# Splitting the value weights among the q products, ones by ScalarE, a padded tile of maxima and a new order at the stage borders of a transformer block

## The chip, the cores and the metric

The kernel runs on one core of a Trainium2 chip. The core has five engines that each work through a queue of their own, in order: TensorE (PE, matrix products; its loads of the stationary operand are listed as PEld), VectorE (DVE), ScalarE (ACT), GpSimd (POOL), and SyncE (SP), which here only issues DMA transfers. ACT issues a few transfers too. Engines wait for each other by semaphores. The metric is the device time of one execution in microseconds; lower is better.

## What is computed

The block is a transformer block on x of 2048 rows by 512 columns, with a condition vector c that modulates both halves. The attention has 32 heads of 16, works in 4 segments of 512 rows, and each segment also reads a memory that the earlier segments wrote.

```python
mod = (_silu(c) @ w_mod).reshape(c.shape[0], 6, 1, -1)
sa, ca, ga, sb, cb, gb = ...
h = _layernorm(x) * (1 + ca) + sa
x = x + ga * _A_ref(h, A_wq, A_wk, A_wv, A_wo, A_beta)
h = _layernorm(x) * (1 + cb) + sb
x = x + gb * _B_ref(h, B_w1, B_b1, B_w2, B_b2)

# _A_ref, for each segment s, with phi(t) = t + 1 where t > 0, else exp(t)
logits = einsum("bhqd,bhkd->bhqk", qs, ks) * scale + mask
a_dot = einsum("bhqk,bhkd->bhqd", softmax(logits), vs)
num = einsum("bhld,bhde->bhle", phi(qs), M)
den = einsum("bhld,bhd->bhl", phi(qs), z)[..., None] + 1e-6
outs.append(g * num / den + (1.0 - g) * a_dot)
M = M + einsum("bhld,bhle->bhde", phi(ks), vs)
z = z + einsum("bhld->bhd", phi(ks))
# then o @ wo

# _B_ref, with 1792 hidden columns
gelu(x @ w1 + b1) @ w2 + b2
```

The mask here is the reference's own: a key after the query gets -1e9.

## The kernel before

The whole order of the work is written out by hand (the scheduler is told to keep program order), so each engine's queue is the program's order.

**Projections, segment by segment.** `PRM["A"]` holds one string of tokens for each of the four segments, and the loop in `block_kernel` that reads it turns each token into steps. `Q0`–`Q3` and `K0`–`K3` are the q and k products of 128 columns each (48 matmuls of 512 columns in three precision terms per four products); `N0`–`N3` are segment 0's q, whose matmuls already ran, so that only their evictions are left. `V0`–`V3` are the value products. `proj` evicts a product: ACT copies it to bf16 (`parts[0]`), DVE subtracts (`r1`), ACT copies the rest (`parts[1]`), POOL makes the third part; where phi is wanted, ACT takes the exponential, POOL (DVE for the fourth k) takes a minimum, and a last DVE step, put off into `late_v`, completes it. The stores of the parts to the DRAM buffers QD and KD are put off into `late_sp` and go out on SP with the next product. `gk`/`gv` copy the high half of a weight block on ACT, `lk`/`lv` subtract the low half on DVE. `s0`–`s3`, `r`, `p0`–`p3` are the LayerNorm of the next segment's x (statistics and normalisation on DVE, the inverse root on POOL). `X` loads x, `W` loads eight blocks of w_mod on SP, `D` is one of the eight steps that multiply and add them (two on ACT, six on DVE). `Tk` transposes phi(k) on PE, `Tc` copies it on ACT, `At` transposes the normalised x, `Ah` scales it on ACT, `H` splits it on DVE, `U` updates the memory. `R` reads the memory (products dn and nu on PE, three DVE steps on dn, four ACT copies), `Rs` stores the reciprocal, `Rm` multiplies on POOL, `Ro` and `Rz` store to AMD on SP. `b` prepares the gates, with 32 small POOL memsets. `B`, in segment 3, allocates the first two stacks (`new_stack`, which writes ones into the last 32 rows of `kst`) and loads them (`load_stacks`). Products share eight PSUM banks in rotation.

**Attention.** The 32 heads of the 4 segments make 64 steps P of two heads; two steps make a group Q of four heads. For each P, PE forms the logits with the query on the partitions (line L607 and, for the small blocks, L640, L641 and the mask product L650), DVE takes their masked maxima (L610, L614) four steps ahead, `m_rows` (L666) splits a group's maxima into three bf16 terms on DVE, `m_put` turns them with one product (L671), ACT copies the result (`ms`) and sends it by DMA into three rows of `qst`, so that the second logit product (L692, keys on the partitions) comes out with the maximum subtracted. ACT takes exponentials (L707, L718), POOL masks the diagonal blocks (L695), and PE multiplies with V (`pv`, L732). Inside a step the order comes from `PRM["order"]`; positions such as `mrows`, `mput`, `mix` are offsets in tenths of a step P from the start of the group (of U, two groups, for `mix`, `olo`, `ohi`). For each U the output goes to DRAM and back (TD, dn, opk), the denominators go through RD and return spread as rbB, `mix` combines them (POOL up to U=13, DVE for 14 and 15), `o_hi` (ACT) and `o_lo` split the result, and `wo_part` multiplies with wo (L809) into the bank `mm`. `wo_out` adds x and stores rows to X2D.

**Feed-forward.** `ffn1(n)` forms one column block of 128 (L982) and applies gelu on ACT (L985); `ffn2(m)` runs four blocks behind (`AHEAD` = 4) and adds into four banks `acc` (L1068). w1 and w2 are loaded and split pair by pair: `stage_w1`, `split_w1`, `stage_w2`, `scale_w2` (w2 times the gate, DVE, L1003), `split_w2` (ACT high half L136, DVE low half L139). The first blocks and the last of the attention are interleaved by hand, with `rest(U, ...)` taking steps that are left over.

Of the kernel before, what the change touches and what calls it, by code (L numbers as in the profile page):

```python
# [8 lines left out]
F32 = mybir.dt.float32  # L9
# [3 lines left out]
ALU = mybir.AluOpType  # L13
# [28 lines left out]
 'mput': [-9, -14, -14, -14],  # L42
# [10 lines left out]
 'mixu': 14,  # L53
 'olou': 14,
# [50 lines left out]
def block_kernel(ctx: ExitStack, tc: tile.TileContext, x, wq, wk, wv, wo, betaq, betam,  # L105
# [57 lines left out]
    def transposed(pl, hp, bank, xh, s, ci, tag, bufs, hbufs=2, ds=range(KB), pss=None, lo=None):  # L163
        hs, ls = [], []
        for d in ds:
            ps = pss[d] if pss else turned(bank(), xh, d)
            h = pl.tile([128, 512], F32, tag=f"{tag}h", bufs=hbufs, name=f"{tag}h{s}_{d}")
            act.activation(h, ps, AF.Identity, bias=cols[:, ci, d:d + 1], scale=cols[:, ci + 1, d:d + 1])
            hh = hp.tile([128, 512], F32R, tag=f"{tag}hh", bufs=bufs, name=f"{tag}hh{s}_{d}")
            if tag == "C0" and s == 0 and d == 0:  # L170
                hp.tile([128, 8], F32, name="cpad1")
            hl = hp.tile([128, 512], F32R, tag=f"{tag}hl", bufs=bufs, name=f"{tag}hl{s}_{d}")
            split(hh, hl, h, lo or v)
            hs.append(hh)
            ls.append(hl)
        return hs, ls
# [7 lines left out]
    def new_stack(i, pl=None):  # L184
        for n, d in (("qst", qst), ("kst", kst)):
            a = {"name": f"{n}{i}"} if pl else {"name": f"{n}{i}", "tag": "wm", "bufs": 4}
            d[i] = (pl or wmp).tile([128, 4, 512], BF16, **a)
        (v if i < 2 else pool).memset(kst[i][96:], 1.0)
# [30 lines left out]
    with ExitStack() as pa:  # L219
# [47 lines left out]
        load_mod((0, 1), (act, sp))  # L267
        wqs = load_w(wp, wq, "wq", "phq")
# [232 lines left out]
        def proj(s, nm, g):  # L501
# [8 lines left out]
            r1 = sa.tile([128, 512], F32, tag="qkr", bufs=2, name=f"{nm}r{s}_{g}")  # L510
            act.activation(parts[0], ps, AF.Copy)
            v.tensor_tensor(out=r1, in0=ps, in1=parts[0], op=ALU.subtract)
            flush(late_v)
            if phi:
                ph = sat(f"ph{nm}", f"{nm}p{s}_{g}")
                act.activation(ph, ps, AF.Exp)
                (v if nm == "k" and g == 3 else pool).tensor_scalar(ph, ph, 1.0, None, op0=ALU.min)
                kw = {}
                if nm == "k":
                    if s not in zss:  # L520
                        zss[s] = sa.tile([128, 4], F32, tag="z", name=f"z{s}")
                    kw["accum_out"] = zss[s][:, g:g + 1]
                late_v.append(lambda: v.scalar_tensor_tensor(ph, ps, 1.0, ph, op0=ALU.add, op1=ALU.max, **kw))
                (phq if nm == "q" else phk)[s, g] = ph
# [38 lines left out]
    ce.tile([128, 16], F32, name="cpad0")  # L563
# [23 lines left out]
    with ExitStack() as pb:  # L587
# [4 lines left out]
        so.tile([128, 8], F32, name="spad")  # L592
# [3 lines left out]
        nms, nss = {}, {}  # L596

# [18 lines left out]
        def s_part(P, part):  # L616
            Q, p = P // 2, P % 2
            if p == 0 and part == 0:
                nms[Q] = sb.tile([128, 3, 16], F32, tag="nm", bufs=4, name=f"nm{Q}")
# [43 lines left out]
        def m_rows(Q):  # L663
            n = nms.pop(Q)
            for c in range(2):
                v.tensor_tensor(out=n[:, c + 1], in0=n[:, c], in1=top(n[:, c]), op=ALU.subtract)  # L666
            nss[Q] = n

        def m_put(Q):
            ns = nss.pop(Q)  # L670
            pe.matmul(mm[:48, :128], top(ns.rearrange("q c n -> q (c n)")), identb, start=True, stop=True)  # L671
            ms = sb.tile([48, 128], BF16, tag="ms", bufs=2, name=f"ms{Q}")
            copy(PRM["mse"], ms, mm[:48, :128])
            act.dma_start(qst[Q % NK][96:99], ms)
# [139 lines left out]
        def wo_x(s, b):  # L814
            xbs[s, b] = so.tile([128, D], F32, tag="xb", bufs=3, name=f"xb{s}_{b}")
            r0 = 512 * s + 128 * b
            sp.dma_start(xbs[s, b], x[r0:r0 + 128, :])
# [138 lines left out]
    with ExitStack() as pc:  # L956
# [65 lines left out]
        for b in range(3):  # L1022
            wo_x(3, b)
# [6 lines left out]
        ffn1(3)  # L1030
# [5 lines left out]
        rest(15, "mem_mix", "mix", "o_hi", "o_lo")  # L1036
        assert not [x for x in left if x[0] != "wo_x"], left
        for b in range(4):
            if b == 3:
                wo_x(3, 3)  # L1040
            wo_part(3, b, 3)
            wo_out(3, b)
        scale_w2(0)
        sostack.close()
        c2 = pc.enter_context(tc.tile_pool(name="c2", bufs=1, reuse_waits="tile"))
        w2t = {f: [c2.tile([128, D], F32R, name=f"w2{i}{f}") for i in "hl"] for f in range(FB - 1, 2, -1)}
# [34 lines left out]
        b2r = []  # L1081
        ln2_load(1)
        for n in range(AHEAD, NSEG * FB + AHEAD):
            s, f = divmod(n, FB)
            m = n - AHEAD
            if m < FB:
                split_w2(m)
# [32 lines left out]
            if n < NSEG * FB:  # L1120
                ffn1(n)
# [59 lines left out]
```

## Time and profile before

| what | us |
|---|---|
| runs before: median of 3 | 851.94 |
| runs before: lowest, highest | 850.7, 856.96 |
| profiled execution, device time | 853.31 |
| profiled execution, span from first to last instruction | 851.6 |
| ACT busy in the span | 360.4 |
| DVE busy in the span | 533.5 |
| mean granted TensorE clock | 0.986 |

The times fall into four stretches that can be told apart in the profile: projections to about 194 us, attention to about 513, the border to the feed-forward to about 555, and the feed-forward to the end. A row of the wait view names the engine that waited, its line, what it waited for, then total us, times and the longest. A timeline row gives start, duration, engine, line, operation, output and inputs, the count of merged instructions, and in brackets the idle time before it and what ended it.

### The profile page before, as it was taken

What the parts mean: (1) busy time and instruction counts of PE and PEld (TensorE: products, weight loads), DVE (VectorE), ACT (ScalarE), POOL (GpSimd) and SP (SyncE); (2) the same over time, 40 slices, a digit from 0 to 9 for tenths busy, and PEclk for the clock granted to TensorE, in tenths of its full rate; (3) what the DMA queues carried; (4) which work ended last, traced back from release to release, by engine and by line L of the source; (5) the groups of instructions that cost most, each with busy time, mean ns of one, the idle gap of its engine ahead of it and who ended that gap; (6) DMA issues with size and microseconds to landing.
All of it is one profiled execution on the core that took longest, in us unless ns stands there. A gap on an engine that the chain in (4) does not pass through costs nothing.

```text
span 851.6 us, 13418 instructions
## 1 busy us (share of the span) xinstructions
PE 818.6 (96%) x4669; PEld 552.9 (65%) x4669; DVE 533.5 (63%) x1432; ACT 360.4 (42%) x730; POOL 281.5 (33%) x449
## 2 busy tenths in 40 slices
PE   8979999988999999999999989799999999999998
PEld 4767786855443445445544547588888888888887
DVE  6586775557899987898788725677543334334213
ACT  4454545432678775676687662113211211111110
POOL 1435448145358544557858571000000000000000
PEclk9999999999799999999999999999999999999999
DMA  9854946486365576656556563733020103002001
GB/s 338 293 164 149 308 154 199 153 274 222 101 179 170 161 217 188 210 177 203 178 170 184 183 191 119 233 118 117 26 99 1 50 0 99 1 0 75 26 1 49
DMA packets 83564, 123.01 MB, mean 144 GB/s; under 512 B 14116, under 2 KB 46244, under 8 KB 82984
## 3 DMA queue, kind: packets, MB, share of 16 engines
q1 hardware_dynamic: 81000, 120.19, 44.4%
q10 hardware_dynamic: 2496, 1.97, 0.7%
q8 instruction: 36, 0.59, 0.3%
q14 instruction: 32, 0.26, 0.1%
HBM read 75.60 MB, written 46.15 MB: 143 GB/s over the span
## 4 chain that ended last, share of the span: by engine, by line
PE 72%; DVE 9%; DMA 6%; issue 5%; POOL 3%; ACT 3%; SPq 1%; ACTq 0%; POOLq 0%; DVEq 0%
PE f1b L982 17%; PE acc L1068 17%; PE pv L732 6%; PE att L692 6%; PE att L607 5%; PE mm L809 4%; DVE att L610 4%; PE q L329 3%; PE k L329 2%; PE v L482 2%; PE nu L452 1%; DMA QD<-q 1%; DMA qst<-ms 1%; PE att L650 1%; PE mp L429 1%
## 5 line engine op out<-in xcount | busy, mean ns | idle before, releaser
L610 DVE CUSTOM_DVE_ANT_0 att<-att,maskb 128x512 f32<-128x512 f32 (+2 forms) x384 | 206.7, 580 | 19.9 <-PE att L607 17.3
L707 ACT ACTIVATE pt<-att 128x512 f32<-128x512 f32 (+1 forms) x256 | 125.9, 554 | 54.9 <-PE att L692 54.3
L985 ACT ACTIVATE gt<-f1b,b1t 128x512 f32<-128x512 f32 x56 | 38.4, 688 | 249.0 <-PE f1b L982 205.5
L695 POOL TENSOR_SCALAR_AFFINE_SELECT pt<-pt 128x256 f32<-128x256 f32 x256 | 100.9, 411 | 100.1 <-ACT pt L707 71.1
L138 DVE CAST gh<-gt 128x512 fp32r<-128x512 f32 x56 | 23.8, 425 | 173.2 <-ACT gt L985 173.2
L692 PE MATMUL att<-qst,kst 99*128 99x512 bf16 (+3 forms) x512 | 108.7, 306 | 5.2 <-ACT pt L718 1.8
L607 PE MATMUL att<-kst,qst 96*128 96x512 bf16 (+2 forms) x384 | 96.8, 334 | 3.3 <-DMA qst<-QD 3.1
L1068 PE MATMUL acc<-w2h,gh 128*128 128x512 f32 (+1 forms) x224 | 87.9, 393 | 3.1 <-ACT w2h L136 3.1
L1068 PE MATMUL acc<-w2l,gh 128*128 128x512 f32 (+1 forms) x224 | 87.4, 390 | 1.0 <-DVE w2l L139 1.0
L732 PE MATMUL pv<-pt,V 128*32 128x512 f32 (+2 forms) x992 | 88.2, 442 | 0.0
L1068 PE MATMUL acc<-w2h,gl 128*128 128x512 f32 (+1 forms) x224 | 86.7, 387 | 0.0
L692 PEld LDWEIGHTS <-kst 99*128 99x128 bf16 x512 | 44.9, 99 | 58.3 <-issue 42.5
L982 PE MATMUL f1b<-hodd,w1h 128*128 128x512 f32 x224 | 74.3, 393 | 0.0
L718 ACT ACTIVATE pt<-att 128x512 f32<-128x512 f32 (+1 forms) x128 | 57.1, 509 | 23.3 <-PE att L607 19.6
L607 PEld LDWEIGHTS <-qst 96*128 96x128 bf16 x384 | 33.7, 99 | 42.9 <-issue 24.4
L151 POOL TENSOR_SCALAR crs<-cmv 128x4 f32<-128x4 f32 x4 | 1.0, 246 | 177.8 <-DVE cmv L148 177.7
L610 DVE DVE_READ_ACCUMULATOR2_ANT nm<- 128x1 f32 x384 | 54.2, 141 | 0.0
L1068 PEld LDWEIGHTS acc<-w2h,gh 128*128 128x128 f32 x224 | 42.5, 190 | 12.0 <-ACT w2h L136 3.5
L1068 PEld LDWEIGHTS acc<-w2l,gh 128*128 128x128 f32 x224 | 42.4, 189 | 10.7 <-DVE w2l L139 1.8
L1068 PEld LDWEIGHTS acc<-w2h,gl 128*128 128x128 f32 x224 | 42.4, 189 | 9.0
L982 PEld LDWEIGHTS f1b<-hodd,w1h 128*128 128x128 f32 x224 | 42.1, 188 | 9.1
L732 PEld LDWEIGHTS pv<-pt,V 128*32 128x32 f32 x992 | 22.2, 108 | 36.7 <-issue 26.9
(216 smaller groups left out, 1607.8 us busy)
## 6 DMA issues: line engine op xcount, KB each, us to landing
kst<-KD SPq DMA_DIRECT2D x32, 384.0 KB
qst<-QD SPq DMA_DIRECT2D x32, 384.0 KB
TD<-ts SPq DMA_DIRECT2D x32, 256.0 KB
QD<-q SPq DMA_DIRECT2D x16, 384.0 KB
KD<-k SPq DMA_DIRECT2D x16, 384.0 KB
wm<-in_wmod SPq DMA_DIRECT2D x20, 256.0 KB
QD<-q SPq DMA_DIRECT2D x16, 256.0 KB
KD<-k SPq DMA_DIRECT2D x16, 256.0 KB
```

The source lines that it names most:

```text
L329: pe.matmul(ps, a[:, k, 128 * g:128 * g + 128], b[k], start=(k == 0 and i == 0), stop=(k == KB - 1 and i == 2))
L607: pe.matmul(ps, q_of(P, h, i), k_of(P, h, 128 * (i + 1)), start=True, stop=True)
L610: v.tensor_tensor_reduce(out=src, in0=src, in1=maskb[:, 512 - n:], scale=-1.0, scalar=-4 * NEG, op0=ALU.add, op1=ALU.min, accum_out=dst)
L692: pe.matmul(ps, k[:99, e, 128 * j:128 * j + 128], q[:99, e, 128 * j:512], start=True, stop=True)
L695: pool.affine_select(out=t, in_=t, pattern=pattern, compare_op=ALU.is_ge, fill=0.0, base=0, channel_multiplier=-1)
L707: act.activation(pt[:, h, :], ps[:, :n], AF.Exp, scale=0.25)
L718: act.activation(pt, pv_, AF.Exp, scale=0.25)
L732: pe.matmul(ps[32 * c:32 * c + 32, lo:hi], V[4 * s + j][:, VW * hd:VW * hd + 32], pt[:, c % 2, lo - o:hi - o], start=start, stop=stop)
L809: pe.matmul(ps, a[:, 128 * b:128 * b + 128], w[:, g, :], start=(g == 0 and i == 0), stop=(g == 3 and i == 2))
L982: pe.matmul(ps, a[:, k, :], b[k], start=(i == 0), stop=(i == 11))
L985: act.activation(g, ps, AF.Gelu_apprx_tanh, bias=b1t[:, f:f + 1])
L1068: pe.matmul((mm if lo else acc[b])[:, lo:hi], a[:, c], w[:, lo:hi], start=(f == 0 and i == 0), stop=(last and i == 2))
```

## The change

The diff below leaves out nothing that changes an instruction; context is shortened. It does the following.

- The string for segment 0 is new: the value weights are split (`gv`, `lv`) among the q products, `W` moves from behind the first q product to behind K1, `X` from behind K1 to behind V0, `s0`–`s3` stand between the k products, V0–V3 come ahead of `Tk`, and seven of the eight `D` steps follow `Tc`.
- In segments 1 and 2 `p3` moves behind `R` and `V0`; in segment 3 `R` moves behind K2, and `Rm` ahead of `Rs` and K3.
- In `proj` the exponential on ACT stands ahead of the copy `parts[0]`.
- `new_stack` writes the ones by ScalarE, from a column of ones read with step 0.
- The tile of maxima has 8 x 16 columns in place of 3 x 16, four fixed tiles whose last five rows are set to 0 once; `m_rows` runs on POOL; `m_put` multiplies with 128 columns in place of 48 and stands two positions later for segments 1 to 3.
- `mix` and `o_lo` of U=13 run on DVE.
- At the border: the fourth block of x is loaded with the other three, into a buffer of the tag `ts`; the last `mix`, `o_hi`, `o_lo` stand ahead of the split of column 3; `scale_w2(0)` stands ahead of the last four parts of wo; `split_w2(0)`, `split_w2(1)` and `ffn1(4)` stand ahead of the load for the second LayerNorm.
- Four padding tiles change size or place.

```diff
- 'mput': [-9, -14, -14, -14],
+ 'mput': [-9, -12, -12, -12],
- 'mixu': 14,
- 'olou': 14,
+ 'mixu': 13,
+ 'olou': 13,
- 'A': ['gk0 gk1 gk2 gk3 lk0 lk1 lk2 lk3 N1 W N0 N3 b N2 K0 gv0 gv1 lv0 lv1 s0 K1 X gv2 gv3 lv2 lv3 s1 K2 s2 s3 r D '
-       'K3 p0 p1 D V0 p2 p3 D D V1 D D V2 D D Tk Tc V3 At Ah H U',
-       'Q0 s0 Q1 E s1 Q2 Es W s2 Q3 s3 r K0 p0 K1 p1 K2 p2 K3 p3 R V0 D V1 X Rs D D V2 Rb D Tk Tc V3 At Ah H U',
-       'Q0 s0 D D Q1 s1 D D Q2 s2 Q3 Rm E s3 r K0 Es p0 K1 El p1 Ro K2 p2 K3 p3 R V0 V1 Rs V2 Rb Tk Tc V3 At Ah H U',
-       'Q0 Q1 B Q2 Q3 K0 K1 R K2 Rs K3 Rm Ro Rz'],
+ 'A': ['gk0 gk1 gk2 gk3 lk0 lk1 lk2 lk3 gv0 lv0 N1 gv1 gv2 lv1 lv2 N0 gv3 lv3 N3 b N2 K0 s0 K1 W s1 K2 s2 K3 '
+       's3 r V0 X p0 V1 p1 p2 p3 V2 V3 D Tk Tc D D D D D D D At Ah H U',
+       'Q0 s0 Q1 E s1 Q2 Es W s2 Q3 s3 r K0 p0 K1 p1 K2 p2 K3 R V0 p3 D V1 X Rs D D V2 Rb D Tk Tc V3 At Ah H '
+       'U',
+       'Q0 s0 D D Q1 s1 D D Q2 s2 Q3 Rm E s3 r K0 Es p0 K1 El p1 Ro K2 p2 K3 R V0 p3 V1 Rs V2 Rb Tk Tc V3 At '
+       'Ah H U',
+       'Q0 Q1 B Q2 Q3 K0 K1 K2 R Rm Rs K3 Ro Rz'],
...
-            if tag == "C0" and s == 0 and d == 0:
-                hp.tile([128, 8], F32, name="cpad1")
...
-        (v if i < 2 else pool).memset(kst[i][96:], 1.0)
+        act.activation(kst[i][96:].rearrange("p e n -> p (e n)"), one[96:].to_broadcast([32, 2048]), AF.Copy)
...
+        wp.tile([128, 24], F32, name="wpad")
...
+            if phi:
+                ph = sat(f"ph{nm}", f"{nm}p{s}_{g}")
+                act.activation(ph, ps, AF.Exp)
             act.activation(parts[0], ps, AF.Copy)
             v.tensor_tensor(out=r1, in0=ps, in1=parts[0], op=ALU.subtract)
             flush(late_v)
             if phi:
-                ph = sat(f"ph{nm}", f"{nm}p{s}_{g}")
-                act.activation(ph, ps, AF.Exp)
                 (v if nm == "k" and g == 3 else pool).tensor_scalar(ph, ph, 1.0, None, op0=ALU.min)
...
-    ce.tile([128, 16], F32, name="cpad0")
+    ce.tile([128, 40], F32, name="cpad0")
...
-        so.tile([128, 8], F32, name="spad")
+        so.tile([128, 16], F32, name="spad")
...
+        nmt = [sb.tile([128, 8, 16], F32, name=f"nm{i}", bufs=1) for i in range(4)]
+        for t in nmt:
+            v.memset(t[:, 3:], 0.0)
...
-                nms[Q] = sb.tile([128, 3, 16], F32, tag="nm", bufs=4, name=f"nm{Q}")
+                nms[Q] = nmt[Q % len(nmt)]
...
-                v.tensor_tensor(out=n[:, c + 1], in0=n[:, c], in1=top(n[:, c]), op=ALU.subtract)
+                pool.tensor_tensor(out=n[:, c + 1], in0=n[:, c], in1=top(n[:, c]), op=ALU.subtract)
...
-            pe.matmul(mm[:48, :128], top(ns.rearrange("q c n -> q (c n)")), identb, start=True, stop=True)
+            pe.matmul(mm[:, :128], top(ns.rearrange("q c n -> q (c n)")), identb, start=True, stop=True)
...
-            xbs[s, b] = so.tile([128, D], F32, tag="xb", bufs=3, name=f"xb{s}_{b}")
+            last = s == 3 and b == 3
+            xbs[s, b] = so.tile([128, D], F32, tag="ts" if last else "xb", bufs=2 if last else 3, name=f"xb{s}_{b}")
...
-        for b in range(3):
+        for b in range(4):
             wo_x(3, b)
...
-        ffn1(3)
+        g3 = ffn1_mm(3)
+        rest(15, "mem_mix", "mix", "o_hi", "o_lo")
+        ffn1_split(3, g3)
         for b in range(4):
             wo_part(3, b, 2)
         stage_w2(0)
         stage_w1(6)
         stage_w2(2)
-        rest(15, "mem_mix", "mix", "o_hi", "o_lo")
+        scale_w2(0)
         for b in range(4):
-            if b == 3:
-                wo_x(3, 3)
             wo_part(3, b, 3)
             wo_out(3, b)
-        scale_w2(0)
         sostack.close()
         c2 = pc.enter_context(tc.tile_pool(name="c2", bufs=1, reuse_waits="tile"))
+        c2.tile([128, 16], F32, name="cpad1")
...
+        split_w2(0)
+        split_w2(1)
+        ffn1(AHEAD)
         ln2_load(1)
         for n in range(AHEAD, NSEG * FB + AHEAD):
             s, f = divmod(n, FB)
             m = n - AHEAD
             if m < FB:
-                split_w2(m)
+                if m > 1:
+                    split_w2(m)
...
             if n < NSEG * FB:
-                ffn1(n)
+                if n > AHEAD:
+                    ffn1(n)
```

## The prediction

> **What bounds the kernel now.** I read the page's busy line, then PE's waits, then PE and its granted clock in stretches (columns: stretch, length, busy time of PE, PEld, DVE, ACT, POOL, then clock, DMA share, GB/s), then the timelines around each wait.
>
> ```profile
> PE 818.6 (96%) x4669; PEld 552.9 (65%) x4669; DVE 533.5 (63%) x1432; ACT 360.4 (42%) x730; POOL 281.5 (33%) x449
> ...
> PE pkt L412 <- DVE kp L523: 3.3, 2, 2.3
> PE v L482 <- ACT wvh L257: 3.2, 2, 2.6
> PE acc L1068 <- ACT w2h L136: 3.1, 1, 3.1
> PE att L607 <- DMA qst<-QD: 3.1, 1, 3.1
> PE att L732 <- POOL pt L695: 2.6, 1, 2.6
> PE dn L444 <- DVE qp L523: 2.5, 1, 2.5
> ...
> PE acc L809 <- ACT oh L130: 1.3, 1, 1.3
> PE acc L1068 <- DVE w2l L139: 1.0, 1, 1.0
> ...
> 45.00:50.00 5.00, 4.71 (x12) 3.03 (x13) 4.85 (x8) 2.27 (x6) 2.33 (x3) 0.66 0.97 334
> ...
> 215.00:220.00 5.00, 5.00 (x20) 2.48 (x19) 4.21 (x16) 3.53 (x8) 1.59 (x4) 0.50 0.01 3
> ...
> 510.00:515.00 5.00, 5.00 (x33) 2.91 (x26) 0.00 (x0) 1.85 (x2) 3.07 (x4) 0.66 0.37 126
> 545.00:550.00 5.00, 5.00 (x17) 3.99 (x17) 3.42 (x7) 0.14 (x1) 0.00 (x0) 0.71 0.96 304
> 555.00:850.00 295.00, 293.28 (x1341) 241.36 (x1339) 120.11 (x221) 48.19 (x73) 4.07 (x5) 1.00 0.14 47
> ```
>
> PE is the bound: 818.6 of 851.6 us busy, and from 555 on, in the feed-forward, full (293.28 of 295). So a microsecond saved before 555 comes off the end. PE idles 33 us in all. The listed waits (total, times, longest) are few, long, and stand where one stage hands over to the next; behind each of 2.5 us and more the clock falls to 0.50–0.71. Those matmuls count as busy but run long. So a removed wait is worth its length and part of the slow stretch behind it.
>
> **The change part by part.** The span before is 851.6, the profiled execution 853.3, the median of the runs 851.9: this execution lies 1.4 above the median, and the sum is made against it.
>
> *First segment.* V's products wait for value weights that ScalarE splits in pairs between the k products.
>
> ```profile
> 39.09 1.14 ACT L257 ACTIVATE wvh<-wvr 128x512 fp32r<-128x512 f32 x2
> ...
> 44.13 1.48 POOL L517 TENSOR_SCALAR kp<-kp 128x512 f32<-128x512 f32 x1 [2.68 <-ACT kp L516]
> 45.58 1.24 POOL L526 TENSOR_TENSOR k<-kr,k 128x512 bf16<-128x512 f32 x1
> ...
> 57.80 1.53 DVE L380 SCALAR_TENSOR_TENSOR wm<-wm,sc,wm 128x512 f32<-128x512 f32 x2
> ...
> 58.65 2.76 PE v L482 x12
> ...
> 66.73 5.62 PE q L329 x24
> ```
>
> The change splits them among the q products: four ACT copies of 0.57 and four DVE subtractions, before V is due. V then follows K without a gap from about 39: four products of 2.76 end at 50. The splits push the q products' evictions (and b's) about 3 us later; PE does not feel it, since the k products have banks of their own. POOL now paces K's evictions: 1.5+1.2 each, so phi of K3 is complete near 50.7, and its transposes, now behind all of V, wait under 1. The transposes of x need p0–p3 on DVE, done near 53.5 (the inverse root on POOL queues behind K3's part), a wait of some 1.4. Between the two stand D steps on DVE's queue: six of 0.77 (the other two on ACT), 4.6 in all, ahead of H. So H starts near 58, the four pairs of H take over 4, and the first q product of segment 1 ends near 63. Today it ends at 66.7+2.8 = 69.5. That is 6.4 gained. The eight W loads (2 MB) leave their early place on SP and now stand behind K0's store, from about 43; at the 334 GB/s of the row above they take 6–8 us and land before D needs them at 51–57. X moves behind V0 on SP and has a segment's time. I take 5.5. Ends: 0 (W or H as late as the waits were) and 9.5 (all of PE's idle time there).
>
> *Exp ahead of Copy; p3 behind R.* ACT issues the same three evictions per product; POOL gets its input one wait earlier and DVE's subtraction starts 0.6 later, within the slack that eight banks give. Segment 1 shows no wait of PE: nothing. In segment 2 the second wait of pkt (3.3 − 2.3 = 1.0) goes, as K3's last step no longer stands behind p3: 1.0 (0 to 1.3).
>
> *Segment 3.* R, moved behind K2, has 2.8 us of k product ahead of dn, which waits 2.5 for phi(q).
>
> ```profile
> 91.36 3.63 PE nu L452 x8
> ...
> 183.26 5.06 PE nu L452 x8
> ...
> L188 DVE MEMSET kst<- x2: 1765/1765/1765, 169.8 to 172.0; 32x2048 bf16 x2
> ```
>
> 2.5, and nu's 5.06 against 3.63 in segment 1 at full clock: 3.9, and 0.4 for the next product's slow start. What R's DVE steps delay now is K3's subtraction only. The ones of kst move to ACT. No row shows ACT on 32x2048; at 0.57 per 512 columns it is at most 2.3, and DVE's 1.77 is the near row; I take 1.8. Two of them hold the eviction of q2 as long as DVE's hold its subtraction today, so they come out even; the ends are a loss of 1 and no gain. The other two fill ACT's idle time ahead of the attention. Sum 4.3 (1.5 to 5).
>
> *Start of the attention.* SP works in order: the stores of Ro wait there for POOL's Rm, behind them K3's store, behind that the stacks of Q=2.
>
> ```profile
> 197.28 5.00 POOL L471 TENSOR_TENSOR am<-am,rb 128x512 f32<-128x512 f32 x4
> ...
> 198.59 6.15 SPq L475 DMA_DIRECT2D AMD<-am  x8
> ```
>
> With Rm on POOL ahead of K3 the eight stores find their data ready, and the stacks are issued some 7 us earlier against the products. The wait of 3.1 goes, and with it the stretch at clock 0.50 behind it; there DVE (4.21 of 5) takes over soon, which caps the gain: 5.0 (3.1 to 6.5).
>
> *Maxima: m_rows on POOL, a 128-column tile, m_put two steps later.*
>
> ```profile
> L666 DVE TENSOR_TENSOR nm<-nm x64: 167/174/1146, 204.4 to 491.0; 128x16 f32<-128x16 f32 x64
> ...
> 252.83 0.24 PE L671 MATMUL mm<-identb,nm 128*48 128x128 bf16 x1
> 261.52 0.24 PE L671 MATMUL mm<-identb,nm 128*48 128x128 bf16 x1
> ...
> 285.25 0.24 PE L671 MATMUL mm<-identb,nm 128*48 128x128 bf16 x1
> 293.32 0.24 PE L671 MATMUL mm<-identb,nm 128*48 128x128 bf16 x1
> ...
> 444.37 0.22 PE L640 MATMUL att<-kst,qst 96*128 96x128 bf16 x1
> 444.43 0.22 PE L641 MATMUL att<-kst,qst 96*128 96x128 bf16 x1
> 444.57 0.24 PE L671 MATMUL mm<-identb,nm 128*48 128x128 bf16 x1
> 444.74 0.28 PE L650 MATMUL att<-maskb,identb 128*128 128x256 bf16 x1
> ...
> 446.44 1.27 POOL L781 TENSOR_TENSOR opk<-opk,rbB 128x512 f32<-128x512 f32 x1 [3.37 <-DMA rbB<-RD]
> ```
>
> DVE loses two steps of 0.17 per Q, and up to 1.1 where something stretches them. The m_put rows are 8.07 apart where PE sets the pace and 8.69 where it doesn't; over the whole attention I put that excess at 5. I take 2.0. The ends are minus 4 (POOL, with 0.1–0.2 more per Q than it has room for) and 5. The 48-column product starts 0.14 behind its neighbour and 0.17 ahead of the next, where two 128-column ones of its length start 0.06 apart: 0.19 too much, 24 times in segments 1 to 3, is 4.6; I take 4.0 (0 to 5). The four memsets of the padding run once, in DVE's idle time. m_put's place two steps later leaves the write of ms about one P, the time it already has in segment 0.
>
> [...]
>
> *End of the attention.* Mix and o_lo of U=13 (three steps of 1.27 on POOL) go to DVE, which is idle there.
>
> ```profile
> 503.91 1.27 POOL L781 TENSOR_TENSOR opk<-opk,rbB 128x512 f32<-128x512 f32 x1 [0.71 <-DMA rbB<-RD]
> 506.56 0.63 ACT L130 ACTIVATE oh<-opk 128x512 fp32r<-128x512 f32 x1 [2.05 <-POOL opk L783]
> ...
> 509.47 3.63 PE L732 MATMUL att<-pt,V 128*32 128x512 f32 x28 [2.56 <-POOL pt L695]
> ```
>
> DVE needs about 1.4 for what takes POOL 2.5, so ACT's copy, and the exponentials queued behind it, come 1.1 sooner, and POOL masks them at once. PE's wait halves, and without the low clock its 28 products need about 2.2: 2.7 (0 to 4.4). Next late is the DMA of rbB.
>
> *First feed-forward columns.*
>
> ```profile
> 542.09 0.69 DVE L826 TENSOR_TENSOR xb<-acc,xb 128x512 f32<-128x512 f32 x1 [3.83 <-DMA xb<-in_x]
> 542.70 1.28 DVE L1003 TENSOR_TENSOR w2r<-w2r,gab 128x512 f32<-128x512 f32 x2
> ```
>
> The fourth x tile gets a buffer of its own and its load goes out with the other three; the scaling (1.28) stands ahead of the four sums on DVE, and the splits of w2 rows 0 and 1 (two ACT, two DVE) ahead of column 4 and of the 1 MB load for LN2. So 3.1 and 1.0 go, the slow stretch at 545 (5 us at 0.71, 1.5), and most of oh's 1.3, as mix(15) no longer waits behind the split of column 3. That split is 2 us later and first read three columns on. 7.0 (3, if w2h's place is still held by a store, to 8).
>
> Sum: 5.5+1.0+4.3+5.0+2.0+4.0+2.7+7.0 = 31.5; 853.3 − 31.5 = 822. The pads move addresses only; I put them at nothing.
>
> **The rivals.**
> (1) Waits move. Segment 0 gains 1, as H stands behind six D; w2h still waits for a store (3 in place of 7); the padding gains 1. Then 31.5 − 4.5 − 4 − 3 = 20: 833. For it: POOL and DVE alternate through all of K's chain.
> (2) Nearly all upper ends: 9.5+1.3+5+6.5+4+5+4.4+8 = 43.7: 809.
> (3) No change to be seen. With DVE relieved, POOL's waits for rbB (3.37 above) pace the attention; at 0.8 per Q they eat 24 of the 31.5: 846. Against it: PE is over 96% busy.
> (4) Slower. POOL works in order: m_rows stands behind a mix that waits for rbB and itself waits for DVE's last maximum, holding the masks behind it; PE stops at m_put. It decides from 31.5/30, about 1.05 us per Q; at 1.5 the time is 853.3 − 29.5 + 45 = 869. Against it: mix stands well over one P ahead of m_rows, POOL is 33% busy, and m_put is later.
> [...]
>
> **How the numbers follow.** Forecast (815–829) 0.50, rival 1 (829–841) 0.22, rival 2 0.14, rival 3 (841–860) 0.09, rival 4 0.05. About 1% is what a measurement of this kernel can tell from no change. Faster by over 1% is below 843: 0.86; within 1%: 0.09; slower 0.05. The range 811 to 841 leaves out rivals 3 and 4 and the end of 2.
>
> **What would show it.** PE's waits on wvh, qst<-QD, qp at dn and w2h are gone, the clock is 1.00 at 45, 215 and 545, m_put rows are near 7.9 apart, and the feed-forward starts 30 us earlier. I am wrong if v or q of segment 1 waits for Ahl or wm, if PE waits at L671, or if slow stretches remain.

## The result, and the profile after

The changed kernel takes 824.84 us (median of 4 runs, 823.21 to 826.43) against 852.2 (median of 4, 850.7 to 856.96): a ratio of 0.967, with a 95% interval of 0.9627 to 0.9712. The profiled execution took 823.21, its span is 821.5. The forecast was 822, its range 811 to 841. The busy line of the page, PE's waits, and PE and its clock by stretches (columns as before):

```profile
PE 803.8 (98%) x4669; PEld 547.5 (67%) x4669; DVE 516.1 (63%) x1373; ACT 368.8 (45%) x734; POOL 286.8 (35%) x508
...
PE att L697 <- DMA qst<-ms: 3.0, 2, 2.4
...
PE att L612 <- DMA qst<-QD: 1.7, 1, 1.7
PE acc L814 <- ACT oh L132: 1.5, 1, 1.5
...
45.00:50.00 5.00, 5.00 (x29) 4.25 (x28) 3.60 (x10) 3.77 (x8) 4.17 (x5) 1.00 0.94 299
195.00:200.00 5.00, 0.94 (x4) 0.33 (x5) 1.95 (x7) 0.60 (x1) 0.42 (x2) 1.00 0.66 172
200.00:205.00 5.00, 4.94 (x24) 2.63 (x22) 3.88 (x14) 3.48 (x8) 1.59 (x4) 0.66 0.00 0
515.00:520.00 5.00, 5.00 (x23) 3.81 (x22) 4.90 (x11) 0.69 (x1) 0.00 (x0) 1.00 1.04 309
520.00:815.00 295.00, 295.00 (x1330) 240.75 (x1329) 122.83 (x229) 49.40 (x75) 4.37 (x6) 1.00 0.15 50
```

PE's idle time fell from 33 us to 17.7 (821.5 − 803.8). The waits on wvh, qp, w2h and w2l are gone, and 45–50 and 515–520 run at full clock. One place of the old kind is left: the stacks at the start of the attention (1.7) and the row of maxima behind them (2.4), 4.1 in all where the kernel before waits 3.1, and after them a stretch at clock 0.66.

Where the gain came from is read from the starts of PE rows in the two timelines. The stages: segment 0 (first q product to the next segment's), segments 1 and 2, segment 3 to the first maxima product, from there to the second, from the second to the last, to the first feed-forward column, to the seventh column (`border` further down), and the rest up to the end of the last PE row.

| stage (us) | before | after | gain |
|---|---|---|---|
| ahead of the first q | 16.26 | 15.78 | 0.5 |
| segment 0 | 50.23 | 41.23 | 9.0 |
| segments 1, 2 | 94.95 | 93.93 | 1.0 |
| segment 3 to first maxima | 44.94 | 40.19 | 4.8 |
| first to second maxima | 12.93 | 12.72 | 0.2 |
| second to last maxima | 275.06 | 268.15 | 6.9 |
| to the first feed-forward column | 18.65 | 15.45 | 3.2 |
| to the seventh column | 42.39 | 36.23 | 6.2 |
| rest of the feed-forward | 292.87 | 294.47 | −1.6 |

The sum is 30.2, as the spans have it (851.6 − 821.5 = 30.1). Forecast were 31.5. Two things do not fit: segment 0 gave 9.0 where 5.5 was forecast, and the start of the attention next to nothing where 5.0 was. And the feed-forward got slower, though nothing in it was changed but addresses.

Of segment 0's 9.0, 1.2 is only lent. The first q product of segment 1 now starts while DVE is still splitting its input, one pair every 1.07, and its 12 matmuls take 4.10 (57.01 to 61.11) in place of 2.89 (66.49 to 69.38). Counted to the end of that product, segment 0 gives 7.8 and segments 1 and 2 give 2.2.

### The profile page after: what moved, and what is told of

Same layout as the page of the kernel before. It is cut to its first block, busy times and chain, and to the rows that moved or that the text cites. A ratio compares the mean times of both kernels' runs of the same rounds, so it can differ in the third digit from the quotient of the medians.

```text
span 821.5 us, 13413 instructions
## 1 busy us (share of the span) xinstructions
PE 803.8 (98%) x4669; PEld 547.5 (67%) x4669; DVE 516.1 (63%) x1373; ACT 368.8 (45%) x734; POOL 286.8 (35%) x508
## 4 chain that ended last, share of the span: by engine, by line
PE 78%; DVE 7%; ACT 4%; POOL 4%; DMA 3%; issue 3%; SPq 0%; DVEq 0%; ACTq 0%; POOLq 0%
PE acc L1074 19%; PE f1b L988 18%; PE pv L737 7%; PE att L697 6%; PE att L612 6%; PE q L330 4%; PE mm L814 4%; DVE att L615 3%; PE k L330 3%; PE v L483 2%; DMA qst<-ms 1%; PE mp L430 1%; DMA rbB<-RD 1%; DMA RD<-dn 1%; ACT ts L132 1%
## 5 line engine op out<-in xcount | busy, mean ns | idle before, releaser
L612 PE MATMUL att<-kst,qst 96*128 96x512 bf16 (+2 forms) x384 | 94.8, 329 | 2.2 <-DMA qst<-QD 1.7
```

Source lines behind the costliest of these rows:

```text
L612: pe.matmul(ps, q_of(P, h, i), k_of(P, h, 128 * (i + 1)), start=True, stop=True)
```

## The experiments

All kernels start from the changed one; the edit names what differs. Their stages, from the same rows of each trace, and the median time (4 runs each, 6 for the last). The runs of one kernel lie 3 to 10 us apart, and each has one trace.

| kernel | seg 0 | 1, 2 | 3 to maxima | 1st to 2nd | to last | to ffn | border | ffn | median |
|---|---|---|---|---|---|---|---|---|---|
| after | 41.23 | 93.93 | 40.19 | 12.72 | 268.15 | 15.45 | 36.23 | 294.47 | 824.84 |
| x1_seg0_old | 47.36 | 92.80 | 39.55 | 11.88 | 270.90 | 15.68 | 36.52 | 294.64 | 830.97 |
| x2_seg3_old | 42.31 | 93.92 | 41.73 | 13.35 | 274.11 | 15.95 | 37.75 | 294.30 | 833.62 |
| x3_rows_dve | 42.32 | 94.07 | 39.55 | 10.18 | 270.57 | 16.56 | 37.40 | 294.29 | 827.68 |
| x4_put48 | 42.31 | 93.95 | 39.84 | 13.10 | 272.78 | 15.58 | 38.47 | 294.29 | 830.09 |
| x5_border_old | 42.34 | 93.99 | 39.55 | 12.37 | 267.98 | 15.94 | 45.07 | 294.29 | 834.2 |
| x6_no_c2pad | 42.48 | 93.94 | 39.54 | 11.11 | 270.69 | 15.50 | 35.56 | 294.80 | 826.52 |
| x7_rs_late | 42.32 | 93.99 | 39.55 | 7.74 | 272.65 | 16.29 | 35.86 | 294.28 | 824.72 |
| x8_rm_early | 41.24 | 94.06 | 39.55 | 7.97 | 271.76 | 15.90 | 36.99 | 294.88 | 823.38 |
| x9_copy_first | 42.41 | 94.32 | 41.20 | 11.12 | 271.81 | 16.71 | 36.26 | 294.47 | 826.35 |
| x11_pads_old | 42.49 | 94.35 | 39.72 | 11.85 | 268.48 | 15.92 | 35.78 | 292.86 | 823.13 |
| x12_rm_wpad | 40.63 | 93.95 | 39.54 | 8.24 | 271.74 | 15.90 | 37.81 | 292.86 | 820.33 |

Stages that an edit doesn't touch show how far an untouched stage scatters: segment 0 lies at 40.6 to 41.2 or at 42.3 to 42.5 (where pkt waits 0.3 to 0.8 for kp), the attention from the first maxima product to the last at 280.3 to 282.9 (268.0 to 271.8 from the second on), the border at 35.6 to 38.5.

The 32 maxima products of the attention leave 31 intervals between them. Summed in groups (the last row gives the range of x1_seg0_old, x5_border_old, x6_no_c2pad and x11_pads_old):

| kernel | 1 | 2 to 5 | 6 to 8 | 9 to 17 | 18 to 20 | 21 to 31 |
|---|---|---|---|---|---|---|
| before | 12.94 | 33.52 | 24.36 | 82.90 | 25.76 | 108.52 |
| after | 12.72 | 32.54 | 23.02 | 81.30 | 25.02 | 106.27 |
| x2_seg3_old | 13.35 | 33.28 | 23.14 | 82.06 | 28.50 | 107.14 |
| x3_rows_dve | 10.19 | 33.23 | 25.09 | 81.31 | 25.54 | 105.39 |
| x4_put48 | 13.10 | 33.79 | 23.09 | 83.38 | 25.20 | 107.31 |
| x7_rs_late | 7.74 | 33.39 | 22.74 | 81.31 | 28.31 | 106.92 |
| x8_rm_early | 7.97 | 32.97 | 22.74 | 81.31 | 27.58 | 107.16 |
| x9_copy_first | 11.12 | 32.43 | 22.74 | 81.36 | 27.75 | 107.52 |
| x12_rm_wpad | 8.24 | 33.02 | 23.11 | 81.36 | 27.69 | 106.56 |
| four others | 11.1–12.4 | 32.8–33.9 | 22.7 | 81.3–81.8 | 24.9–26.1 | 106.0–107.0 |

**Segment 0 ordered as before** (x1_seg0_old).

```diff
- 'gk0 ... lk3 gv0 lv0 N1 gv1 gv2 lv1 lv2 N0 gv3 lv3 N3 b N2 K0 s0 K1 W s1 K2 s2 K3 s3 r V0 X p0 V1 ...'
+ 'gk0 ... lk3 N1 W N0 N3 b N2 K0 gv0 gv1 lv0 lv1 s0 K1 X gv2 gv3 lv2 lv3 s1 K2 s2 s3 r D K3 p0 p1 ...'
```

> The changed kernel with segment 0 ordered as before: the first value weights split in pairs among the k products, W early, X behind K1. Theory (segment 0 gave 9 us, where the prediction had 5.5): the first q product of segment 1 starts near 66 in place of 57, the v wait on wvh of 2.6 is back, everything later moves by the same 9, and the time is near 824.8 + 9 = 834. Rival (part of the 9 came from the other edits in the segment, Exp ahead of Copy, which stay in): the first q product of segment 1 starts at 62 to 63 and the time is near 830.

The rival held: segment 0 takes 47.36, 4.9 to 6.1 more than with the new order (3.6 to 4.9 counted to the end of segment 1's first q product) and 2.9 less than before the change; the time is 830.97. POOL's first minimum of k, in the timelines of the kernel before and of this one:

```profile
38.76 1.50 POOL L517 TENSOR_SCALAR kp<-kp 128x512 f32<-128x512 f32 x1 [0.76 <-ACT kp L516]
```

```profile
36.37 1.50 POOL L519 TENSOR_SCALAR kp<-kp 128x512 f32<-128x512 f32 x1
```

With the exponential ahead of the copy it starts 2.4 earlier (2.2 counted from the first q product) and no longer waits for ACT. So the 9.0 is the new order (5 to 6) and about 3 that other edits give in the old order too. Which of them gives it was not separated; the exponential's place is the likely one.

**Copy ahead of the exponential** (x9_copy_first), the segment strings new.

```diff
+            act.activation(parts[0], ps, AF.Copy)
+            v.tensor_tensor(out=r1, in0=ps, in1=parts[0], op=ALU.subtract)
             if phi:
                 act.activation(ph, ps, AF.Exp)
-            act.activation(parts[0], ps, AF.Copy)
-            v.tensor_tensor(out=r1, in0=ps, in1=parts[0], op=ALU.subtract)
```

> The changed kernel with the Copy ahead of the exponential on ACT in every projection's eviction, as before; the segment strings stay new. Theory (the run with segment 0's old order kept 2.9 of that segment's gain, and there POOL's minimum of k, which needs the exponential, started 2.4 earlier): the first q product of segment 1 starts 2 to 3 later against the first q product of segment 0 (41.2 to 42.3 in the changed kernel), segment 2 loses up to 1, time 827.5 to 829. Rival (the prediction's 0 in segment 0: the eight banks hide the order, and the 2.9 came from the pads or the tile of ones): no shift in segment 0, time 824.8 to 826.

The rival held for segment 0 (42.41, as in most runs), and the loss turned up elsewhere: 0.4 in segment 2 and 1.0 to 1.7 in segment 3, where PE now waits for DVE's subtraction; 826.35. In segment 0 the two edits are not additive: pkt waits 2.3 for kp in the kernel before, 0.9 with the old order alone (x1_seg0_old) and 0.8 with the copy first alone, so either one takes most of the same wait.

```profile
PE mm L483 <- DVE kr L513: 1.1, 1, 1.1
```

**Segment 3 ordered as before** (x2_seg3_old).

```diff
- 'Q0 Q1 B Q2 Q3 K0 K1 K2 R Rm Rs K3 Ro Rz'
+ 'Q0 Q1 B Q2 Q3 K0 K1 R K2 Rs K3 Rm Ro Rz'
```

> The changed kernel with segment 3 ordered as before: R ahead of K2, Rs ahead of K3, Rm and its eight stores behind K3. Theory (the reorder alone carries segment 3 and what the start of the attention gave): dn waits 2.5 again and nu runs near 5, so K3's products end 4 to 5 later against the start of segment 3; the first att wait on the stacks grows back from 1.7 to about 3; together 5 to 6, a time near 830. Rival (the late stacks come from the volume of the stores alone, not from their order): the wait at the first att product stays near 1.7 and the whole difference is the 4 of dn and nu, near 829 with Q=2's first maxima at most 4.5 later.

Both fell short: 833.62, 8.8 more. Waits of PE, then two stretches of this kernel:

```profile
PE att L612 <- DMA qst<-QD: 4.1, 1, 4.1
PE dn L445 <- DVE qp L525: 1.0, 1, 1.0
...
200.00:205.00 5.00, 3.03 (x9) 1.26 (x10) 2.19 (x7) 1.23 (x3) 0.37 (x1) 0.51 0.67 166
...
362.00:364.00 2.00, 2.00 (x9) 0.20 (x8) 1.52 (x7) 0.30 (x1) 1.04 (x4) 0.50 1.01 294
```

Only 1.5 to 2.2 of it lies in segment 3, where dn waits 1.0 in place of the 2.5 of the kernel before. The stacks' wait is 4.1, with the clock at 0.51 around it, and from the second maxima product to the last it takes 2 to 6 more, a second stretch at half clock at 362 included. That stretch, 3 us of intervals 18 to 20, is not the order's alone: x9_copy_first, with the new order, has one too. So in this trace most of what the new order of segment 3 is worth lies in the attention, and in segment 3 itself it is worth less than forecast.

**Row subtractions on DVE again** (x3_rows_dve).

```diff
-                pool.tensor_tensor(out=n[:, c + 1], in0=n[:, c], in1=top(n[:, c]), op=ALU.subtract)
+                v.tensor_tensor(out=n[:, c + 1], in0=n[:, c], in1=top(n[:, c]), op=ALU.subtract)
```

> The changed kernel with the two row subtractions of the maxima on DVE again, the padded tile and the later product kept. Theory (the prediction's m_rows term, 2.0, is real and separate from the padding): from the first to the last maxima product of the attention 1.5 to 2 us longer than in the changed kernel, time near 826.5. Rival (the padding gave all of the 6.0 seen there): no difference, the same spacing of 7.9 to 8.0 of the products, time 824.8 within 0.7.

From the first maxima product to the last it is 280.75, against 280.87, as the rival had it; the median, 827.68, is 2.8 higher, nearer to the theory. Two differences hide in the sum. Intervals 6 to 8 take 25.09 here and 24.36 in the kernel before, against 22.7 to 23.1 in every kernel of the table with the subtractions on POOL. There DVE's subtraction stands until POOL's split of wo has ended:

```profile
240.36 1.35 DVE L671 TENSOR_TENSOR nm<-nm 128x16 f32<-128x16 f32 x2
240.40 1.28 POOL L863 TENSOR_TENSOR wol<-wor,woh 128x512 fp32r<-128x512 f32 x1
```

The second of these two subtractions takes 1.14, where the median is 0.175, and ends with POOL's row. It happens in four groups here and in the kernel before (there 1.34 to 1.35 for the two, at 248.93, 257.65, 266.35 and 275.04), and none of POOL's subtractions in the changed kernel takes over 0.43. So the move to POOL is worth about 2 in that place, as the theory had it. Against it, interval 1 is 0.9 to 2.5 shorter here than in the kernels that leave the start of the attention alone, and intervals 21 to 31 are 0.6 to 2.1 shorter; whether that belongs to the edit stays open.

**A product of 48 columns from the padded tile** (x4_put48).

```diff
-            pe.matmul(mm[:, :128], top(ns.rearrange("q c n -> q (c n)")), identb, ...)
+            pe.matmul(mm[:48, :128], top(ns[:, :3].rearrange("q c n -> q (c n)")), identb, ...)
```

> The changed kernel with the maxima product of 48 columns, read from the padded tile, so that the product's width alone differs. Theory (0.19 too much at each of the products in segments 1 to 3, by the starts of the neighbouring rows): 4 to 4.6 longer between Q2's and Q31's maxima products, a time near 829. [...] Second rival (the six us of the attention came from DVE's relief alone): no difference.

The theory held: 285.88 from the first maxima product to the last, 5.0 more than in the changed kernel and 3.0 more than the highest of those that leave the attention alone; 830.09. The same place in the timelines of the changed kernel and of this one:

```profile
301.25 0.38 PE L612 MATMUL att<-kst,qst 96*128 96x256 bf16 x2
301.48 0.22 PE L676 MATMUL mm<-identb,nm 128*128 128x128 bf16 x1
301.53 0.71 PE L697 MATMUL att<-qst,kst 99*128 99x256 bf16 x5
```

```profile
305.22 0.38 PE L612 MATMUL att<-kst,qst 96*128 96x256 bf16 x2
305.53 0.24 PE L676 MATMUL mm<-identb,nm 128*48 128x128 bf16 x1
305.70 0.72 PE L697 MATMUL att<-qst,kst 99*128 99x256 bf16 x5
```

From the row ahead to the row behind it takes 0.28 with 128 columns and 0.48 with 48: 0.20 a product, 4.8 for 24. The intervals agree: 13 to 16 take 10.6 each before and with 48 columns, 10.4 in the changed kernel and in x3_rows_dve. The weights' loads of these products take 101 ns for 48 columns in the kernel before and 98 ns for 128 in the changed kernel, so they don't explain it.

**The border ordered as before** (x5_border_old): all of the border's edits undone, the pads kept; the core of it:

```diff
-            last = s == 3 and b == 3
+            last = False
...
-        scale_w2(0)
...
         for b in range(4):
+            if b == 3:
+                wo_x(3, 3)
             wo_part(3, b, 3)
             wo_out(3, b)
+        scale_w2(0)
...
-        split_w2(0)
-        split_w2(1)
-        ffn1(AHEAD)
         ln2_load(1)
```

> The changed kernel with the order of before at the border to the feed-forward: the last x tile loads into a buffer that is still in use, its wo products and sums stand behind column 3, scale and splits of w2 and column 4 as before. Theory (the border gave 6.1): the waits of acc on w2h (3.1) and w2l (1.0) are back, the clock falls behind them, and from the first feed-forward column to the end of the second w2 row it takes 6 us more; time near 831. Rival (what feeds w2h stands so much earlier in the changed kernel that the old order costs only its own waits, not the low clock): 3 to 4 more, near 828.5.

It costs 8.8 at the border and 9.4 in all (834.2), more than the 6.2 that the change gained there. The same two waits come back, 0.6 and 0.9 longer than in the kernel before:

```profile
PE acc L1075 <- ACT w2h L138: 3.7, 1, 3.7
...
PE acc L1075 <- DVE w2l L141: 1.9, 1, 1.9
```

What each of the border's edits is worth by itself was not separated.

**The stacks' place in SP's queue**, in x7_rs_late

```diff
- 'Q0 Q1 B Q2 Q3 K0 K1 K2 R Rm Rs K3 Ro Rz'
+ 'Q0 Q1 B Q2 Q3 K0 K1 K2 R Rm K3 Rs Ro Rz'
```

and in x8_rm_early

```diff
- 'Q0 Q1 B Q2 Q3 K0 K1 K2 R Rm Rs K3 Ro Rz'
+ 'Q0 Q1 B Q2 Q3 K0 Rm K1 Ro K2 R K3 Rs Rz'
```

> The changed kernel with Rs, the store of the reciprocals, moved in segment 3 from ahead of K3 to behind it. Theory (SP stands blocked at Rs until DVE's reciprocals are done at 179.5, and K2's store, the sums' stores and the stacks wait behind it): the K2 store leaves SP about 3 us earlier, the first attention products no longer wait for the stacks (1.7) and less for the maxima's row (2.4), and Q=2's first maxima come 2 to 4 earlier; time near 822. Rival (the stacks are late by the volume of the stores ahead of them, some 5 MB): no change in the first attention waits, time 824.8 within 1; or, as the broadcast of the reciprocals comes later, Rm stands and the attention starts up to 2 later.

> The changed kernel with two of the four Rm steps and their stores in segment 3 moved ahead of the K1 and K2 steps. These read what the segment before left, so their data are as ready as in segment 3's later place only if the reciprocals of that segment are: theory (the volume of the stores, 1 MB of sums among them, stands ahead of the stacks): 1 MB goes out while the DMA engines stand idle, the stacks land about 3 earlier, the waits of 1.7 and 2.4 fall below 1, time near 822. Rival (SP's order, not the volume, holds the stacks): no change there, 824.8 within 1, or K1's and K2's evictions on POOL stand behind the moved steps and segment 3 gets 1 to 2 longer.

SP's timeline of the kernel before, then of the changed one, then of x7_rs_late:

```profile
207.31 0.73 SPq L193 DMA_DIRECT2D kst<-KD  x1
```

```profile
179.55 0.33 SPq L461 DMA_DIRECT2D rdd<-rd  x1
179.98 2.33 SPq L500 DMA_DIRECT2D KD<-k  x3
182.40 5.15 SPq L476 DMA_DIRECT2D AMD<-am  x8
187.64 2.45 SPq L500 DMA_DIRECT2D KD<-k  x3
190.19 0.61 SPq L193 DMA_DIRECT2D kst<-KD  x1
```

```profile
180.02 0.33 SPq L461 DMA_DIRECT2D rdd<-rd  x1
180.44 5.05 SPq L476 DMA_DIRECT2D AMD<-am  x8
185.59 2.46 SPq L500 DMA_DIRECT2D KD<-k  x3
188.14 0.62 SPq L193 DMA_DIRECT2D kst<-KD  x1
```

In the kernel before the stacks go out 45.87 after segment 3's first q product (207.31 − 161.44), in the changed one 39.25 after it (190.19 − 150.94). That is 6.6 earlier; but PE reaches the first maxima product 4.8 earlier too (44.94, 40.19), so against the products it is 1.9 only. SP is free of Rm, but stands at Rs, whose data DVE delivers at 179.5, and behind it the stores of K2, of the sums and of K3. With Rs behind K3 the stacks go out 35.18 after it (188.14 − 152.96), and the stage to the second maxima product falls from 12.72 to 7.74. So the theory of x7_rs_late held for that place: the queue's order held the stacks, and it frees the 5 us that had been forecast there. x8_rm_early has Rs behind K3 too, and besides stores 1 MB of the sums earlier. Its stacks go out after 35.83 (186.64 − 150.81) and the stage takes 7.97, no less than with Rs alone. So its theory, the volume, is not shown; the order alone is enough for both.

But the totals hardly move (824.72 and 823.38): from the second to the last maxima product it takes 4.5 and 3.6 more than in the changed kernel, where kernels that leave the attention alone lie up to 3.7 above it. Some 3 of it is one stall in intervals 18 to 20. In x8_rm_early, rows of POOL, ACT and PE near 350, then three stretches of it:

```profile
345.61 1.27 POOL L786 TENSOR_TENSOR opk<-opk,rbB 128x512 f32<-128x512 f32 x1 [2.70 <-DMA rbB<-RD]
...
348.26 0.63 ACT L132 ACTIVATE oh<-opk 128x512 fp32r<-128x512 f32 x1 [1.92 <-POOL opk L788]
...
349.32 0.27 PE L697 MATMUL att<-qst,kst 99*128 99x128 bf16 x2 [0.89 <-ACT pt L712]
...
348.00:350.00 2.00, 0.96 (x6) 0.47 (x6) 1.15 (x5) 1.74 (x4) 2.00 (x5) 1.00 0.59 147
350.00:352.00 2.00, 1.67 (x6) 0.45 (x4) 1.78 (x5) 2.00 (x6) 2.00 (x6) 0.62 0.68 211
352.00:354.00 2.00, 2.00 (x10) 0.20 (x8) 1.60 (x7) 0.38 (x1) 1.04 (x4) 0.52 1.00 277
```

mix waits 2.7 for rbB, ACT's copy behind it 1.9, the exponentials stand behind the copy, PE waits 0.9, and then runs at about half clock for some 3 us. In x7_rs_late the place is the same and the form another: PE waits 2.16 for a stack. Its SP rows, then PE's:

```profile
332.09 0.42 SPq L570 DMA_DIRECT2D xt<-X2D  x1
...
335.59 0.49 SPq L193 DMA_DIRECT2D qst<-QD  x1
337.81 0.34 SPq L775 DMA_DIRECT2D RD<-dn  x1
344.61 0.59 SPq L781 DMA_DIRECT2D rbB<-RD  x1
...
344.47 0.60 PE L612 MATMUL att<-kst,qst 96*128 96x512 bf16 x2 [2.16 <-DMA qst<-QD]
```

The stack went out at 335.59, 9 us before PE gets it, behind the 1 MB load of x for the second LayerNorm (332.09), and the store RD behind it (337.81) lands no sooner, as the start of rbB's load shows, which waits for it. rbB's load goes out at 344.61, after PE's wait has ended, so it is not what held the stack up. Nor is the stall shown to be the price of the gain ahead: x12_rm_wpad has it, but so do x9_copy_first and x2_seg3_old, whose start of the attention is not early, while the changed kernel and six others do not have it.

**The load of rbB later** (x10_rb_late), from x8_rm_early.

```diff
- 'rbl': 7,
+ 'rbl': 13,
```

> The kernel with two Rm steps and their stores moved ahead, and besides the load of rbB placed 0.6 of a step P later, behind the stacks in SP's queue. Theory (the 5.5 gained at the start of the attention is given back near 340 to 355 because SP stands at rbB's load, 4 to 6 us for RD, with a stack behind it): the stall there and the half clock behind it vanish, from the first maxima product to the last 2.5 to 4 less, time near 820. Rival (mix on POOL then waits for rbB and holds the masks behind it): POOL's waits for rbB grow from 7 to over 15 and PE waits for the masks, time 825 to 835.

The rival held in POOL's waits for rbB, and far beyond its numbers; but PE stands for the exponentials, not for the masks: 880.61, a ratio of 1.0324 to the kernel before (1.0254 to 1.0393). POOL's waits in x8_rm_early, then in this one, then PE's in this one:

```profile
POOL opk L786 <- DMA rbB<-RD: 7.0, 4, 2.7
```

```profile
POOL opk L786 <- DMA rbB<-RD: 59.6, 11, 7.4
...
PE att L697 <- ACT pt L712: 35.1, 12, 4.5
```

Moved by 0.6 of a step, the load makes POOL wait 11 times in place of 4, and the chain shown for x8_rm_early repeats through the attention: 57 us. So rbB has next to no room. Whether an earlier load would remove the stall in intervals 18 to 20 was not tried.

**The pads** (x6_no_c2pad, x11_pads_old, x12_rm_wpad).

x6_no_c2pad leaves out the first tile of this list, x11_pads_old makes all of the edits, and x12_rm_wpad makes all but the last, from x8_rm_early.

```diff
-        c2.tile([128, 16], F32, name="cpad1")
...
-    ce.tile([128, 40], F32, name="cpad0")
+    ce.tile([128, 16], F32, name="cpad0")
...
-        so.tile([128, 16], F32, name="spad")
+        so.tile([128, 8], F32, name="spad")
...
+                hp.tile([128, 8], F32, name="cpad1")
...
-        wp.tile([128, 24], F32, name="wpad")
```

> The changed kernel without the pad tile of c2 ahead of the feed-forward's buffers. Theory (the second feed-forward product's blocks of 2.80 against 2.76 before come from the addresses that the pads moved): the blocks return to 2.76 and the time falls by 1 to 2, to 823. Rival (the longer blocks come from something else, as the loads that run beside them): blocks of 2.80 stay and the time stays 824.8 within 0.7.

> The changed kernel with the four pad tiles at the sizes and places of before; the tile of maxima stays padded, so the addresses behind it are not all those of before. Theory (the 2.80 in place of 2.76 of the second feed-forward product's blocks hangs on addresses that these pads move): blocks of 2.76, the feed-forward 1.5 shorter, and some change of up to 1 in the q and k products of the projections. Rival (it comes from elsewhere): 2.79 to 2.80 as in the changed kernel, time 824.8 within 1.

> The kernel with two Rm steps and their stores moved ahead (823.4), with the pad ahead of wq kept and the other three pad tiles as before. Theory (the pad ahead of wq is what shortens the q and k products, the other three are what lengthen the second feed-forward product): q and k of segment 0 take 11.3 and 11.0 as in the changed kernel and not 11.5 and 11.25, the second product's blocks take 2.76, and the time is 1.5 to 2 lower, near 821.5. Rival (one pad does both, as all later addresses hang on it): either q and k take 11.5 and 11.25 again, or the blocks stay at 2.79 to 2.80; time near 823.4.

Without the c2 pad alone nothing changes (294.80). With the pads of before the feed-forward is back at 292.86 (292.87 in the kernel before). From the starts in the timelines, a block of 12 w2 products takes 2.80 in the changed kernel and 2.76 in x12_rm_wpad:

```profile
573.01 0.39 PE L1074 MATMUL acc<-w2h,gh 128*128 128x512 f32 x1
...
575.81 0.39 PE L988 MATMUL f1b<-hodd,w1h 128*128 128x512 f32 x1
```

```profile
572.26 0.40 PE L1075 MATMUL acc<-w2h,gh 128*128 128x512 f32 x1
...
575.02 0.40 PE L990 MATMUL f1b<-hodd,w1h 128*128 128x512 f32 x1
```

And the pad ahead of wq does the opposite in the projections. The first q, k and v products of segment 0, in x11_pads_old and in x12_rm_wpad:

```profile
16.47 0.47 PE L331 MATMUL q<-Ahh,wqh 128*128 128x512 f32 x1
...
27.98 0.39 PE L331 MATMUL k<-Ahh,wkh 128*128 128x512 f32 x1
...
39.23 0.40 PE L484 MATMUL v<-wvh,Ahh 128*128 128x512 f32 x1
```

```profile
15.73 0.47 PE L332 MATMUL q<-Ahh,wqh 128*128 128x512 f32 x1
...
27.00 0.39 PE L332 MATMUL k<-Ahh,wkh 128*128 128x512 f32 x1
...
37.99 0.39 PE L485 MATMUL v<-wvh,Ahh 128*128 128x512 f32 x1
```

q and k take 11.51 and 11.25 without it, 11.27 and 10.99 with it: 0.5. So the theory held: the pads act apart from each other, and x12_rm_wpad takes the better of each. Which of the three lengthens the feed-forward was not separated. Its time: 820.33 (817.16 to 826.85), a ratio of 0.9632 to the kernel before (0.9589 to 0.9674). That is the lowest median here; its interval overlaps the changed kernel's.

## Why the prediction held, point by point

The forecast, 822 against 824.84, came out of a sum of 31.5 against 30.1, and some of that agreement is luck: the start of the attention gave 4.8 less than forecast, and segment 0 with segments 1 and 2 gave 3.5 more.

- **The bound.** Right: PE's idle time fell by 15.3 (33 to 17.7) and its busy time by 14.8 (818.6 to 803.8), with the slow stretches and the narrow products. A wait was worth its length and more.
- **Segment 0: 5.5, measured 9.0 (7.7 to 9.6 over the other kernels with the new order).** The mechanism was right and its size short. The forecast's own difference of 6.4 compared the ends of segment 1's first q product; counted so, it is 7.8 (6.5 to 8.4). The chain ran earlier than drawn up: p0–p3 end at 52.0 in place of 53.5, and H starts at 56.4 in place of "near 58". "Segment 1 shows no wait of PE: nothing", in the part on the exponential, holds beside the new order (x9_copy_first loses nothing in segment 0), but in the old order the other edits give 2.9 there, of which the pad ahead of wq has about 0.5.
- **Exponential ahead of the copy and p3: 1.0, measured 1.0 in segments 1 and 2.** That the two agree is luck: the 1.2 lent to segment 0 is taken off here, and behind it the gain is 2.2. It holds pkt's second wait of 1.0, as forecast, 0.4 that x9_copy_first gives back, 0.4 that x11_pads_old gives back, and 0.4 that stays open.
- **Segment 3: 4.3, measured 4.8.** Right in size and not in cause. The forecast had R's place for all of it; with R in its old place the segment is already 3.2 shorter than before (44.94 to 41.73), 1.5 of it in dn's wait, which is 1.0 there and not 2.5; R's place adds 1.5 to 2.2. Which edits give the 3.2 was not separated. The copy put first again costs 1.0 to 1.7 of this segment (x9_copy_first), which the forecast didn't have. The ones of kst took ACT 1.90 each against an estimate of 1.8.
- **Start of the attention: 5.0, measured 0.2 up to the second maxima product.** This is the term that failed, in the step "the stacks are issued some 7 us earlier against the products. The wait of 3.1 goes". They were issued 1.9 earlier against them. Ro's stores no longer wait for POOL, but SP now waits at Rs for DVE, and R's own place behind K2 makes that data late: Rs goes out 28.6 after the segment's first q product, 25.1 with the old order (x2_seg3_old). The mechanism, a store that holds up the stacks, was right, and so was the price: 5.0 with Rs behind K3 (x7_rs_late). The list of what SP meets on the way was one entry short.
- **Maxima: 2.0 + 4.0, measured 6.9.** The padding carries 4.6 to 4.8, as 0.19 times 24 had it. The subtractions on POOL are worth about 2 in intervals 6 to 8, by the stretching to 1.1 that the forecast had read; the total of x3_rows_dve doesn't show it. The later place of the product was not tried alone.
- **End of the attention: 2.7, measured 3.2,** in a stage that scatters by 1.3, and not tried alone. **Border: 7.0, measured 6.2;** what is left there is oh's wait of 1.5.
- **The pads: nothing, measured a loss of 1.6 in the feed-forward and a gain of 0.5 in the q and k products of segment 0.** "The pads move addresses only" was right and not a reason for nothing.

By the prediction's own signs, the waits on wvh, qp and w2h are gone, the one on qst<-QD is not, and a slow stretch remains behind it. None of the three places that the first rival named gave way: segment 0 and the padding gained more than forecast, and w2h's wait is gone. What moved was the wait at the start of the attention, which it didn't name. The mechanism of the third rival, POOL's waits for rbB, exists and is near: x10_rb_late made it decide, at 0.6 of a step. The fourth rival's stop at m_put is not seen there: PE waits 1.1 in all for POOL's rows of maxima.

## What to carry to other kernels

When a store is moved out of a DMA queue's way, write down everything that is left between the queue's head and the transfer that matters, each with the time at which its data are ready; the next entry takes over at once (here Rs, at which SP waited 4.4). Measure a stage to the end of the first work behind it as well as to its start, since a start that comes early may run slowly (segment 1's first q product took 4.10 in place of 2.89). Look into a sum by intervals before calling two kernels the same: here a loss of 2 stood beside a gain of the same size. And undo each edit alone: here two edits covered the same wait, and four tiles that hold nothing cost the feed-forward 1.6.

## What had not been expected of the hardware

- A product with 48 stationary columns among products of 128 cost 0.20 us more than one of 128 (x4_put48 and the changed kernel: 0.48 against 0.28 from the row ahead to the row behind).
- FP32 products of one shape differed by 1 to 2% in spacing with the pads, which move nothing but addresses: 2.80 against 2.76 for 12 of w2 (the changed kernel, x12_rm_wpad), 11.51 against 11.27 for the 48 of q (x11_pads_old, x12_rm_wpad).
- Some 1.4 us without a product in 4 us (0.96 and 1.67 busy of 2.00 each), the longest wait 0.89, came with about half the clock in x8_rm_early near 350 (0.62, then 0.52), and intervals 18 to 20 took 27.58 there against 25.02 in the changed kernel, so a wait under 1 us can cost more than its length. It doesn't always: from 506 to 510 in the changed kernel PE is idle for 1.8 and the clock stays at 1.00.
- A DVE subtraction of 128x16 whose median is 0.175 takes 1.14 while POOL works on wol, and ends with it (x3_rows_dve, 240.36).
